# A recurrent-memory attention with a routed MLP on one core: the first step's softmax, left rows and a granule's load rearranged, and the tail's gate and up products turned round

## The chip, the core and the metric

The kernel runs on one core of a Trainium2 chip. Its engines are TensorE (PE in the profile; PEld is its weight load), VectorE (DVE), ScalarE (ACT), GpSimd (POOL) and SyncE (SP), which here only issues DMAs. The metric is the device time of one execution in microseconds; less is better. The time of a kernel is the median of several executions.

## The reference

Inputs are bfloat16. Part A is attention over 64 segments of 32 rows, with 8 memory rows that each segment hands to the next; part B is an MLP on the two rows that a router picks. Cut to what matters:

```python
def _A_ref(x, mem0, Wq, Wk, Wv, Wo, seg_len):   # x (1, 2048, 1024), 32 heads of 128, M = 8 memory rows, seg_len = 32
    ...
    for s in range(n_seg):
        xs = x[:, s * seg_len:(s + 1) * seg_len, :].copy()
        h = jnp.concatenate([mem, xs], axis=1)
        q = jnp.einsum('btd,dhe->bhte', h, Wq)
        ...
        p = _softmax(scores, axis=-1)
        o = jnp.einsum('bhqk,bhke->bhqe', p, v)
        o = jnp.einsum('bhte,hed->btd', o, Wo)
        mem = o[:, :M, :].copy()
        outs.append(o[:, M:, :])
    return jnp.concatenate(outs, axis=1)
def _B_ref(x, w_r, w_gate, w_up, w_down):       # w_gate, w_up (1024, 3584), w_down (3584, 1024)
    ...
    x_sel = jnp.take_along_axis(x, idx_e, axis=1)
    g = _silu(x_sel @ w_gate)
    u = x_sel @ w_up
    y = g * u @ w_down
    ...
xn = _layernorm(x, axis=-1)
return x + _A_ref(xn, A_mem0, A_Wq, A_Wk, A_Wv, A_Wo, A_seg_len) + _B_ref(xn, B_w_r, B_w_gate, B_w_up, B_w_down)
```

## The kernel before

**Main and left rows.** Only what the recurrence needs goes from segment to segment: 8 memory rows and the first 24 rows of the segment, 32 rows in all (ST, one column per row). The last 8 rows of each segment, 512 rows over the 64 segments, are the left rows. They change nothing for the memory, so their queries, keys and values are worked out together in the first segment, dense and 128 wide, their attention runs along with the segments, and their output projection comes in the tail.

**Weights.** Wq, Wk, Wv and Wo are cut into 64 granules of 128 x 2048 (512 KB): 0 to 47 for six phases of q, k and v (PHASES, line 27), 48 to 63 for Wo. 44 granules are resident in SBUF. 17 are streamed again for every segment through five slots (`fetch`, line 383, tile g, queue SP); three more are partly kept in PSUM (KEPT) and brought back by copies. Some rooms are used twice. The room "pair" first holds XLT, the turned left rows; later granules 60 and 61. "big0" holds the raw left rows XLR, then gathered queries and keys (GA), then W8A, then OTA, the left rows' attention output. "big1" holds x, then GA, then W8B, eight granules of Wo. The room of granule 62 (`hm`) holds VG, the left values, in between.

**The start** (lines 619 to 631). `left_stats` takes mean and variance of four tiles of 128 left rows on VectorE and normalises them; `left_turns` transposes them on TensorE, eight blocks a tile, into XLT; `left_qk` then makes a head's queries with eight matmuls of 512 columns (line 506) and ScalarE copies them to GA (line 508). The weights of the first phase come in two halves (`first_half`, line 460).

**The first segment.** Each phase is followed by the same product for the left rows. After a phase of v, `left_v` (line 527) runs four tiles of rows times four column blocks, each of eight matmuls (line 533), copies each block to VG (line 536, ScalarE and VectorE in turn) and stores it to vl_d in HBM (line 537, SP). In the second half it also loads W8B through POOL, and granule 60 once the first two tiles of XLT are used. `scores` (QK products, mask, maximum) is run by a hook at a point of the phases; `exponent` (ScalarE, line 681) and `soften` (VectorE) follow at a later hook. In the first segment the second half's pair stands at hook (4, 7), the last block of phase 4, ahead of VM's copy (line 785) on ScalarE. At a phase's end `left_done` (line 554) fetches the streamed granules that follow and, after phase 5, loads 61 and 62.

**The segments.** Six phases, then the residual (line 358) and sixteen granules of Wo (line 804). PSm's matmuls (line 757) hold 32 columns of weights (ST) and are placed in four column groups of the array, so that four run side by side.

**The tail.** During the last segment's Wo the parts of OTA that the first two blocks of left rows need are loaded (eight loads of 256 KB, `load_left_out`, on POOL), and with each Wo granule one piece of the MLP's weights is fetched (`fetch_moe`, SP, 16 pieces of gate). Then six pieces of up go out and the other eight loads of OTA (SP); the left x rows are loaded on ScalarE's queue. `left_sums` normalises those on VectorE, `left_rows_out(0)` and `(1)` each project two blocks of 128 left rows (64 matmuls of 512 columns a block, line 880, in PSUM WD), add x (line 886) and store them (line 887, POOL). Between the two, `gate_up(0, early)` multiplies the first 20 of 32 pieces, and the rest after. A piece of weights is the stationary operand, 14 blocks of 128 x 128, and the two routed rows are the moving one, two columns wide (line 910); the freed room takes the next piece. Then silu (928), the product (930), and 112 matmuls with w_down (938) into YP. T is the two routed output rows, loaded back from HBM after the left rows are stored (923); line 941 adds YP to them and line 943 stores them.

**Order.** The order of each engine is the order of the program text (`manual_schedule`); each queue's DMAs are issued in that order too. The hardware queues of SP and ScalarE share eight semaphores, so a ninth DMA waits for the first to land.

## Time and profile before

| | us |
|---|---|
| median of 3 runs | 1842.9 (1832.21 to 1852.85) |
| the profiled execution | 1829.7 |
| its span, first to last instruction | 1828.1 |
| PE busy | 1552.2 (85%) |
| DVE, ACT, POOL busy | 878.1, 776.9, 321.0 |
| mean granted PE clock | 0.986 |
| moved by DMA | 678.50 MB, mean 371 GB/s |

All rows of the profile are from one execution. "L506" is line 506. A row of the timeline has the start, the length, engine, line, operation, out<-in, the size and how many were merged, and in brackets the idle time before it with what ended it. A row of a line's or group's view gives count, shortest, median and longest duration in ns and the first and last start. A queue row gives a DMA's form, how many, their size and the median time from issue to landing. The first segment reaches to about 226, the last segment's Wo ends at 1743.8, and the tail is what follows.

### The profile page before, as it was taken

What the parts mean: (1) busy time and instruction counts of PE and PEld (TensorE: products, weight loads), DVE (VectorE), ACT (ScalarE), POOL (GpSimd) and SP (SyncE); (2) the same over time, 40 slices, a digit from 0 to 9 for tenths busy, and PEclk for the clock granted to TensorE, in tenths of its full rate; (3) what the DMA queues carried; (4) which work ended last, traced back from release to release, by engine and by line L of the source; (5) the groups of instructions that cost most, each with busy time, mean ns of one, the idle gap of its engine ahead of it and who ended that gap; (6) DMA issues with size and microseconds to landing.
All of it is one profiled execution on the core that took longest, in us unless ns stands there. A gap on an engine that the chain in (4) does not pass through costs nothing. (4 is left out here: it accounts for less than half of the span.)

```text
span 1828.1 us, 70401 instructions
## 1 busy us (share of the span) xinstructions
PE 1552.2 (85%) x30370; PEld 827.1 (45%) x30370; DVE 878.1 (48%) x2707; ACT 776.9 (42%) x2023; POOL 321.0 (18%) x596
## 2 busy tenths in 40 slices
PE   6999888888888888888888888888888888888888
PEld 3444344444444444444444444444444444444465
DVE  6722254555455555544555455454445555555420
ACT  2342144444444444444444444444444444444400
POOL 1111111111111111111111111111111111111200
PEclk9999899999999999999999999999999999999988
DMA  9785999999999999999999999999999999999996
GB/s 360 274 302 158 308 364 369 395 391 397 375 393 395 395 396 393 379 387 368 397 394 398 384 389 396 369 382 379 383 393 395 395 389 396 397 395 395 389 385 246
DMA packets 219961, 678.50 MB, mean 371 GB/s; under 512 B 46849, under 2 KB 50225, under 8 KB 219649
## 3 DMA queue, kind: packets, MB, share of 16 engines
q1 hardware_dynamic: 193688, 623.79, 89.0%
q0 software_dynamic: 24512, 47.59, 7.6%
q8 instruction: 237, 3.88, 0.9%
q10 hardware_dynamic: 1448, 2.62, 0.4%
q14 instruction: 76, 0.61, 0.1%
HBM read 652.90 MB, written 29.89 MB: 374 GB/s over the span
## 5 line engine op out<-in xcount | busy, mean ns | idle before, releaser
L757 PE MATMUL PSm<-wres,ST 128*32 128x512 bf16 x6400 | 499.9, 382 | 0.0
L757 PEld LDWEIGHTS <-ST 128*32 128x32 bf16 x12288 | 312.3, 96 | 336.7 <-issue 91.4
L757 PE MATMUL PSm<-g,ST 128*32 128x512 bf16 x3080 | 307.1, 384 | 37.0 <-DMA g<-wsc 33.7
L414 ACT COPY BK<-KEPT 128x512 bf16<-128x512 bf16 x315 | 189.2, 601 | 180.3 <-PE WO L804 68.2
L804 PEld LDWEIGHTS <-OT 128*32 128x32 bf16 x8192 | 209.3, 97 | 88.6 <-issue 72.2
L766 ACT CAST XB<-PSm 128x512 bf16<-128x512 f32 x256 | 150.2, 587 | 118.8 <-PE PSm L757 117.4
L804 PE MATMUL WO<-W8B,OT 128*32 128x256 bf16 x4096 | 186.8, 277 | 0.0
L654 DVE COPY KT<-BT 128x512 bf16<-128x512 bf16 x126 | 51.1, 405 | 280.8 <-PE BT L644 276.2
L757 PE MATMUL PSm<-W8A,ST 128*32 128x512 bf16 x2048 | 182.8, 381 | 0.0
L599 POOL DMA_DIRECT2D QKL<-ql_d x63 | 46.5, 737 | 753.3 <-ACT OTL L726 738.5
L804 PE MATMUL WO<-g,OT 128*32 128x256 bf16 x2560 | 130.7, 277 | 55.6 <-DMA g<-wsc 50.1
L838 POOL DMA_DIRECT2D out_dram<-XN x256 | 130.6, 525 | 178.3 <-DVE XN L834 177.9
L785 ACT CAST VM<-PSm 128x512 bf16<-128x512 f32 x128 | 80.1, 625 | 114.3 <-PE PSm L757 114.3
L414 DVE COPY BK<-KEPT 128x512 bf16<-128x512 bf16 x189 | 80.2, 425 | 72.3 <-ACT BK L414 36.6
L644 PEld LDWEIGHTS <-XB 128*128 128x128 bf16 x1024 | 58.0, 98 | 108.7 <-ACT XB L766 102.0
L644 PE MATMUL BT<-IDENT,XB 128*128 128x128 bf16 x1024 | 101.7, 222 | 3.3
L686 DVE TENSOR_REDUCE DN<-BS 128x8 f32<-128x320 f32 x128 | 62.9, 492 | 85.4 <-ACT BS L681 85.4
L671 DVE TENSOR_TENSOR BS<-BS,CT 128x96 f32<-128x96 f32 (+1 forms) x256 | 59.7, 233 | 84.3 <-PE BS L664 79.8
L506 PE MATMUL PSG<-XLT,wres 128*128 128x512 bf16 x352 | 98.7, 382 | 0.8 <-ACT GA L508 0.7
L649 ACT COPY QT<-BT 128x512 bf16<-128x512 bf16 x128 | 74.9, 585 | 52.7 <-PE BT L644 49.2
L757 PE MATMUL PSm<-BK,ST 128*32 128x512 bf16 x567 | 75.3, 387 | 22.5 <-DVE ST L372 22.5
L834 DVE CAST XN<-WO 128x256 bf16<-128x256 f32 x64 | 27.2, 425 | 131.7 <-PE WO L804 131.7
(176 smaller groups left out, 2282.1 us busy)
## 6 DMA issues: line engine op xcount, KB each, us to landing
g<-wsc SPq DMA_DIRECT2D x1071, 512.0 KB, 6.3
ql_d<-GA POOLq DMA_DIRECT2D x16, 512.0 KB, 6.7
QKL<-ql_d POOLq DMA_DIRECT2D x63, 128.0 KB, 6.2
MW<-in_B_w_gate_dram SPq DMA_DIRECT2D x16, 448.0 KB, 8.3
MW<-in_B_w_down_dram SPq DMA_DIRECT2D x14, 512.0 KB, 10.9
wres<-in_A_Wk_dram SPq DMA_DIRECT2D x12, 512.0 KB, 10.7
MW<-in_B_w_up_dram SPq DMA_DIRECT2D x12, 448.0 KB, 9.6
XP<-in_A_x_dram SPq DMA_DIRECT2D x8, 512.0 KB, 10.5
```

Source lines behind the costliest of these rows:

```text
L414: copy(out=back[g][c], in_=KEPT_COLS[g][c])
L506: nc.tensor.matmul(PSG[:, :], lhsT=part(Gs[kc], h // 4)[:, P * (h % 4):P * (h % 4 + 1)], rhs=XLT[:, :, kc, :], start=(kc == 0), stop=(kc = ...
L644: nc.tensor.transpose(out=PTq[:, il, :, :].rearrange("p j r -> p (j r)"), in_=XB[:, il * P:(il + 1) * P], identity=IDENT[:, :])
L649: nc.scalar.copy(out=QT[half][:, :, :], in_=pv)
L654: (nc.vector.tensor_copy if s else nc.scalar.copy)(out=KT[half][:, :, 0:32], in_=pv)
L671: nc.vector.tensor_tensor(out=S4, in0=S4, in1=m, op=ALU.add)
L686: nc.vector.tensor_reduce(out=DN[:, :], in_=S8, axis=AX.X, op=ALU.add)
L757: nc.tensor.matmul(PSm[32 * jq:32 * jq + 32, :], lhsT=ST[:, kc, :], rhs=part(Gv, jq), start=(kc == 0), stop=(kc == KC - 1), tile_position= ...
L766: nc.scalar.copy(out=XB[:, :], in_=PSm[:, :])
L785: nc.scalar.copy(out=VM[half][:, :], in_=PSm[:, :])
L804: nc.tensor.matmul(PS[32 * g:32 * g + 32, 0:256], lhsT=lhs(h), rhs=Gv[:, D * hs + 256 * g:D * hs + 256 * (g + 1)], start=False, stop=(last ...
L838: nc.gpsimd.dma_start(out=out2[s * SEG:s * SEG + XM, 256 * g:256 * (g + 1)], in_=OB[32 * g:32 * g + XM, :])
```

## The change

In the start the left rows go in two pairs: `left_stats` and `left_turns` take a range, and `first_heads` makes the queries of the first four heads in two column halves of 256, in four banks of PSUM (FIRST) that later hold KEPT. `warm_up` runs matmuls on the identity whose result nothing reads: 80 ahead of the first pair, 24 ahead of the second pair's transposes.

In the first segment the second half's `exponent` and `soften` move from hook (4, 7) into `left_v(0)`, after its first tile of rows. In `left_v(1)` the stores of the last two tiles go through POOL, and granule 61 is loaded in two halves, after the third and the fourth tile, where before it followed phase 5.

In the tail four of POOL's eight loads of OTA, and the left x, move to SP, behind the segment's loop and ahead of the remaining fetches. Gate and up hold the two routed rows (RX, padded to 32 columns) as the stationary operand and stream the weights, 448 columns a matmul, in four column groups; the result lies across 32-row groups in four banks, silu and product work on four parts, and seven transposes (HTP) bring it back to columns. w_down is loaded in an order that fits them. `keep_warm` runs 12 and 5 more matmuls that nothing reads. A silu on one unused column is placed ahead of `left_rows_out(1)`.

```diff
+    def warm_up(n):
+        W = psA.tile([P, 512], F32, tag="acc", name="WARM")
+        for _ in range(n):
+            nc.tensor.matmul(W[:, 0:P], lhsT=IDENT[:, :], rhs=IDENT[:, :], start=True, stop=True)
+
+    def first_heads(Gs, c):
+        for h in range(4):
+            for kc in range(KC):
+                nc.tensor.matmul(FIRST[h][:, 256 * c:256 * (c + 1)], lhsT=part(Gs[kc], 0)[:, P * h:P * (h + 1)],
+                                 rhs=XLT[:, 2 * c:2 * c + 2, kc, :], start=(kc == 0), stop=(kc == KC - 1), skip_group_check=True)
+            if c == 1:
+                GA = gathered[0].rearrange("p s (m i q r) -> p s m i q r", m=2, i=4, q=4)
+                nc.scalar.copy(out=GA[:, :, 0, h, 0, :], in_=FIRST[h].rearrange("p (s r) -> p s r", r=XL))
...
-    moe += [("dn", fg) for fg in range(FC // 2)]
+    moe += [("dn", j, gp) for j in range(FC // 4) for gp in range(2)]
...
+                W = B_w_down.rearrange("(f g x) d -> f g x d", f=2, g=4)
+                for f in range(2):
+                    x0, x1 = max(P * j, FQ * f), min(P * (j + 1), FQ * (f + 1))
+                    if x0 < x1:
+                        nc.sync.dma_start(out=t3[x0 - P * j:x1 - P * j, :, :],
+                                          in_=W[f, 2 * gp:2 * gp + 2, x0 - FQ * f:x1 - FQ * f, :].rearrange("a p d -> p a d"))
...
-    def left_v(half, Gs):
+    def left_v(half, Gs, amid=()):
...
-                nc.sync.dma_start(out=vl_d[b][4 * jq:4 * jq + 4, :, :, half, :].rearrange("i s r e -> (s r) i e"),
-                                  in_=VQ.rearrange("p (i e) -> p i e", i=4))
+                (nc.gpsimd if half and b > 1 else nc.sync).dma_start(
+                    out=vl_d[b][4 * jq:4 * jq + 4, :, :, half, :].rearrange("i s r e -> (s r) i e"), in_=VQ.rearrange("p (i e) -> p i e", i=4))
             nc.gpsimd.tensor_copy(out=GATE, in_=VG[:, 1536:1540])
+            if b == 0:
+                for fn in amid:
+                    fn()
...
+                if b > 1:
+                    g = AREAS["pair"][1]
+                    c = slice(D * (b - 2), D * (b - 1))
+                    res_tiles[g] = room(g, "")
+                    nc.sync.dma_start(out=res_tiles[g][:, c], in_=granule_dram(g)[:, b - 2, :])
...
-            for g in AREAS["pair"][1:] + [hm]:
-                load_resident(g)
+            load_resident(hm)
...
-    left_stats()
-    left_turns()
+    warm_up(80)
+    left_stats(0, 2)
+    left_turns(0, 2)
+    first_heads(first_Gs, 0)
+    left_stats(2, 4)
+    warm_up(24)
+    left_turns(2, 4)
     row_stats(xt(0), S6, MV[:, 0, :])
     sd_rows(MV[:, 0:1, :], VE[:, 0:1])
-    left_qk(0, 0, [t for _, t in first_phase], iter(()), 0, 2)
+    gathered[0] = area("big0", [P, NSEG, 256], "GA")
+    first_heads(first_Gs, 1)
     spread(0, 1)
     norm_seg(0)
-    left_qk(0, 0, [t for _, t in first_phase], iter(()), 2, 5)
+    left_qk(0, 0, first_Gs, iter(()), 4, 5)
...
-        hook(*((5, 0) if s else (4, 7)), exponent)
-        hook(*((5, 0) if s else (4, 7)), lambda: soften(1))
+        if s:
+            hook(5, 0, exponent)
+            hook(5, 0, lambda: soften(1))
...
-                    left_v(half, [Gv_ for _, Gv_ in behind])
+                    left_v(half, [Gv_ for _, Gv_ in behind], () if half else (exponent, lambda: soften(1)))
...
-                for k in range(8):
+                for k in range(4):
                     load_left_out(k, nc.gpsimd)
...
-    fetch_moe()
-    for k in range(8, 16):
+    for k in range(4, 8):
         load_left_out(k, nc.sync)
...
-        nc.scalar.dma_start(out=left_x(t), in_=x_left[t, :, XM:SEG, :])
+        nc.sync.dma_start(out=left_x(t), in_=x_left[t, :, XM:SEG, :])
+    fetch_moe()
+    for k in range(8, 16):
+        load_left_out(k, nc.sync)
...
+    GU = [[psA.tile([P, 512], F32, tag="acc", name=f"GA{fh}") for fh in range(2)], [BS, BT]]
+    RX = T2[:, 256:512].rearrange("p (k r) -> p k r", r=32)
+    nc.vector.memset(T2[:, 256:512], 0.0)
+    nc.vector.tensor_copy(out=RX[:, :, 0:2], in_=RXT)
...
-            for fl in range(FC // 2):
-                col = (w * FC + fh * (FC // 2) + fl) * 2
-                nc.tensor.matmul(GU[:, col:col + 2], lhsT=Gt[:, fl * P:(fl + 1) * P], rhs=RXT[:, kc, :],
-                                 start=(w + kc + fh + fl == 0), stop=True, skip_group_check=True)
+            for g in range(4):
+                nc.tensor.matmul(GU[w][fh][32 * g:32 * g + 32, 0:FQ], lhsT=RX[:, kc, :], rhs=Gt[:, FQ * g:FQ * (g + 1)],
+                                 start=(kc == 0), stop=(kc == KC - 1), tile_position=(0, 32 * g), skip_group_check=True)
...
     gate_up(0, early)
+    nc.scalar.activation(out=T2[:, 126:127], in_=T2[:, 124:125], func=ACTF.Silu)
     left_rows_out(1)
...
+    keep_warm(12)
+    HTP = psA.tile([P, 1024], BF16, tag="acc", name="HTP")
+    for j in range(FC // 4):
+        nc.tensor.transpose(out=HTP[:, P * j:P * (j + 1)], in_=HR[:, P * j:P * (j + 1)], identity=IDENT[:, :])
...
+    keep_warm(5)
```

More of the change, by code (lines that the diff above doesn't have):

```diff
@@ L499, in left_qk @@
     def left_qk(mat, half, Gs, between, h0=0, h1=16):
-        if mat == 0 and h0 == 0:
+        if mat == 0 and half and h0 == 0:
             gathered[half] = area(f"big{half}", [P, NSEG, 256], "GA")
@@ L872, with keep_warm @@
     OTR = OTA.rearrange("p s (r h) -> p (s r) h", h=H)
+    def keep_warm(n):
+        W = psK.tile([P, 512], F32, name="WARM", tag="kept0")
+        for i in range(n):
+            nc.tensor.matmul(W[:, 0:256], lhsT=IDENT[:, :], rhs=T2[:, 256:512], start=True, stop=True)
     def left_rows_out(k):
@@ L891 @@
     left_rows_out(0)
-    ROW = T0[:, 0:256]
+    T3 = one.tile([P, 256], BF16, tag="bA", name="T3")
+    ROW = T3[:, 0:256]
     def quarters(c):
-        return T0[c:c + 97:32, 0:256]
+        return T3[c:c + 97:32, 0:256]
     def routed_out(v):
@@ L926 @@
     end_rows = [ends[c].value_load(I8[0:1, c:c + 1], min_val=0, max_val=S - 1) for c in range(2)]
[L927 to L930 removed]
+    HR = T0[:, 0:2 * FQ]
+    SG = [[T0[:, 1024 + 448 * i:1024 + 448 * (i + 1)].bitcast(F32) for i in range(2)],
+          [one.tile([P, 224], F32, tag=tag, name="SG") for tag in ("kt", "bE")]]
@@ L931 @@
+    HT = T2[:, 160:160 + 2 * FC].rearrange("p (j g c) -> p j g c", g=4, c=2)
+    nc.vector.tensor_copy(out=HT, in_=HTP[:, 0:32 * FC].rearrange("p (j g r) -> p j g r", g=4, r=32)[:, :, :, 0:2])
+    keep_warm(5)
     YP = psA.tile([P, 512], F32, tag="acc", name="YP")
     nc.vector.memset(YP[:, 0:256], 0.0)
-    for fg in range(FC // 2):
-        Gt = moe_tiles["dn", fg]
-        for a in range(2):
-            fc = 2 * fg + a
-            for g in range(4):
-                nc.tensor.matmul(YP[32 * g:32 * g + 2, 0:256], lhsT=HT[:, fc, :],
-                                 rhs=Gt[:, a * D + 256 * g:a * D + 256 * (g + 1)], start=(fc == 0), stop=(fc == FC - 1),
-                                 tile_position=(0, 32 * g))
+    for j in range(FC // 4):
+        for gp in range(2):
+            Gt = moe_tiles["dn", j, gp]
+            for a in range(2):
+                for g in range(4):
+                    nc.tensor.matmul(YP[32 * g:32 * g + 2, 0:256], lhsT=HT[:, j, 2 * gp + a, :],
+                                     rhs=Gt[:, a * D + 256 * g:a * D + 256 * (g + 1)], start=(j + gp + a == 0),
+                                     stop=(j == FC // 4 - 1 and gp + a == 2), tile_position=(0, 32 * g))
```

50 lines of the change are left out of this document (28 added, 22 removed).

## The prediction

> **What bounds the kernel now.** I read the page first: the span, the DMA's share in its slices, the chain of waits.
>
> ```profile
> span 1828.1 us, 70401 instructions
> ...
> DMA  9785999999999999999999999999999999999996
> ...
> DMA g<-wsc 4%; PE PSm L757 1%; PE WO L804 1%; DMA VL<-vl_d 0%; PE YP L938 0%; DMA out_dram<-XLS 0%; PE BT L644 0%; ACT QT L649 0%; ACT BS L681 0%; DVE DN L686 0%; DVE KT L654 0%; DVE PT L692 0%; DVE XN L834 0%; DVE PT L696 0%; PE BS L662 0%
> ```
>
> The largest piece of the chain is the streamed weights (g<-wsc), and the DMA is full in nearly all slices. Busy time by stretches shows where it isn't (columns: stretch, length, five engines, PE clock, DMA share, GB/s):
>
> ```profile
> 212.00:216.00 4.00, 2.94 (x89) 2.26 (x89) 2.80 (x12) 1.36 (x5) 0.69 (x2) 1.00 0.66 136
> 408.00:600.00 192.00, 161.96 (x3592) 86.28 (x3596) 97.81 (x313) 89.25 (x240) 35.39 (x64) 1.00 1.02 390
> 1763.00:1773.00 10.00, 10.00 (x50) 6.63 (x49) 0.09 (x1) 0.00 (x0) 0.47 (x1) 1.00 1.03 407
> ```
>
> The loop over segments streams at 390 GB/s with a full DMA, and the change leaves it alone. In the first segment, where the left rows are done too, the DMA has slack and TensorE sets the time: 216 us is where the stream becomes the bound, so what TensorE saves before it shifts all that follows. In the tail both are full. What TensorE waits for between 60 and 300 us (total, times, longest):
>
> ```profile
> PE WO L804 <- DMA g<-in_A_Wo_dram: 4.0, 2, 3.7
> PE PSV L533 <- ACT VM L785: 2.2, 1, 2.2
> ```
>
> **The start.** Two rows of the left pairs are to be normalised, turned and multiplied before the other two.
>
> ```profile
> L240 DVE BATCH_NORM_AGGREGATE MISC<-MISC x4: 209/209/209, 5.7 to 10.4; 128x2 bf16<-128x12 f32 x4
> ```
> ```profile
> L232 PE MATMUL PX<-IDENT,XLR x32: 267/314/315, 11.9 to 15.6; 128*128 128x128 bf16 x32
> ```
> ```profile
> 17.04 1.01 PE L506 MATMUL PSG<-XLT,g 128*128 128x512 bf16 x2 [1.10 <-ACT XLT L233]
> 17.84 1.06 PE L506 MATMUL PSG<-XLT,wres 128*128 128x512 bf16 x2
> ```
> ```profile
> L508 ACT CAST GA<-PSG x4: 585/585/586, 20.3 to 25.6; 128x512 bf16<-128x512 f32 x4
> ```
> ```profile
> 8.19 0.33 SPq L460 DMA_DIRECT2D wres<-in_A_Wq_dram  x1
> ```
> ```profile
> wres<-in_A_Wq_dram SPq DMA_DIRECT2D x1, 256.0 KB, 5.6
> ```
>
> Before, the fourth head is through at 25.6. After, the second aggregate comes at 5.7 + 1.57 = 7.3, the first turn 1.5 later as before (10.4 to 11.9), at 8.8. But the last half granule, issued at 8.19, lands at 13.8, and that holds all heads: 25 half-wide matmuls then remain. At full clock one 512-wide matmul costs 13.60/64 = 0.21 (left rows, below), so half costs 0.106: to 16.5. The 24 warm-up matmuls, a quarter each, add 1.3; turning and copying the second pair half of the 5.1 that four took (11.9 to 17.04), 2.6; 32 more half-wide ones 3.4: 23.8, and 0.3 for the spread that the old order had already passed. Gain 1.5. VectorE's second pair (3.1 of statistics and about 1.5 to the turn, after its copy at about 11.5) is ready at 16 to 17, under TensorE's work. The matmuls at 17 us come two in 0.80, half the full rate. If that clock still held, 57 half-wide ones would cost 0.094 more each: the gain would be a loss of 3.9. If the 24 fell under a wait, it would be 2.8. I take 1.5, since 80 warm-up matmuls precede.
>
> The Trainium skill (TensorE: Matmul & The Clock Gate, Part 1) says that about 3.4 us of activity release the full clock and an idle window of that length takes it away; by it the wait until 13.8 is just short enough and 1.5 stands, and the half-rate pair at 17 us agrees with it.
>
> **The softmax moved.** VM's copy no longer stands behind the exponent on ScalarE, and the 2.2 above goes. Exponent and divisions now stand between ScalarE's and VectorE's copies of left v; each of them copies one product in two, so the work fits in the 3.4 between its copies (two products of 8 x 0.21). If it didn't, it would give back at most the 2.2.
>
> **The stores on POOL and granule 61.**
>
> ```profile
> 207.88 0.58 ACT L536 CAST VG<-PSV 128x512 bf16<-128x512 f32 x1 [5.49 <-DMA vl_d<-VG]
> ```
> ```profile
> 213.39 3.29 SPq L389 DMA_DIRECT2D g<-in_A_Wo_dram  x3
> ```
> ```profile
> 211.75 0.38 PE L533 MATMUL PSV<-g,XLT 128*128 128x512 bf16 x1
> ```
> ```profile
> 224.41 0.62 PE L804 MATMUL WO<-wres,OT 128*32 128x256 bf16 x8 [0.73 <-DMA wres<-in_A_Wo_dram]
> ```
>
> SP's three fetches stood behind the last stores of v and started 1.4 after TensorE had freed the room. Now only half a granule stands there (0.4): 1.0 sooner. Half of 61 leaves this busy stretch: 256 KB at 390 GB/s, 0.7. The load of 62 into VG's room still waits for the last stores. The ScalarE wait at 207.88 stays, since the store now queues on POOL behind three loads of 512 KB. So 1.7 (0 to 2.7, the upper end with that wait shortened by 1.0). New waits: POOL's stores wait for the copies of v, and behind them stand W8B's last two loads and the next segment's QKL, none of them needed before 213; the second half of 61 waits on SP for TensorE's last columns of x, and behind it stand the three fetches (its 0.4 is counted). First segment: 1.5 + 2.2 + 1.7 = **5.4**.
>
> **The tail's loads.**
>
> ```profile
> 1743.11 0.62 PE L804 MATMUL WO<-g,OT 128*32 128x256 bf16 x8 [2.75 <-DMA g<-wsc]
> ```
> ```profile
> OTA<-ol_d POOLq DMA_DIRECT2D x8, 256.0 KB, 9.7
> MW<-in_B_w_gate_dram SPq DMA_DIRECT2D x3, 448.0 KB, 13.9
> XLS<-in_A_x_dram ACTq DMA_DIRECT2D x4, 256.0 KB, 12.6
> ```
> ```profile
> L441 SPq DMA_DIRECT2D MW<-in_B_w_gate_dram x16: 327/330/642, 1733.7 to 1758.6; - x16
> ```
> ```profile
> 1743.66:1759.11 15.45, 15.45 (x64) 9.36 (x65) 0.89 1.04 365
> 1759.11:1772.71 13.60, 13.60 (x64) 9.03 (x63) 1.00 1.03 407
> 1781.24:1796.67 15.43, 15.43 (x65) 9.38 (x65) 0.89 1.04 399
> 1796.67:1810.40 13.73, 13.73 (x65) 9.08 (x63) 1.00 1.01 377
> ```
>
> The last granule shares the DMA with POOL's and ScalarE's loads and lands at 1743.1. With 2 MB of those moved I take 1741.5 (between 1739 and 1743). But four loads of OTA and the left x now stand on SP behind sixteen gate loads, which the segment's loop issues first. At 407 GB/s those 7.34 MB take 18.0 and 1.05 MB of OTA 2.6: OTA is whole at 1762.1. The first row block runs 1742.1 to 1757.5 and TensorE then waits 4.6; the second, cold again, takes 15.45: 1777.6, against 1772.7. The left x land 2.6 after OTA, and their sums, about 10 by the rows (12.6 after some 1738 to VectorE's first sum, at 1761.34 below), end by 1775, under the second block. Behind these loads on SP stand six up pieces and the other eight of OTA: the bytes before them are the same as before, and they are due only at 1783, so nothing is booked for them.
>
> **Gate and up.**
>
> ```profile
> 1761.34 1.28 DVE L886 TENSOR_TENSOR XLS<-XLS,WD 128x512 bf16<-128x512 bf16 x2
> ```
> ```profile
> 1772.71:1781.24 8.53, 7.51 (x282) 0.79 1.04 396
> ```
> ```profile
> 1652.40 1.26 PE PSm L757 x20
> ```
> ```profile
> 1812.05 0.53 POOL L887 DMA_DIRECT2D out_dram<-XLS  x1 [13.28 <-DVE T L921]
> 1816.74 1.23 POOL L923 DMA_DIRECT2D T<-out_dram  x2 [4.16 <-DVE T L930]
> ```
> ```profile
> out_dram<-XLS POOLq DMA_DIRECT2D x4, 256.0 KB, 5.7
> T<-out_dram POOLq DMA_DIRECT2D x2, 2.0 KB, 2.7
> ```
> ```profile
> 1822.74 0.48 DVE L941 SCALAR_TENSOR_TENSOR T<-YP,SIG,T 128x256 bf16<-128x256 f32 x1 [5.77 <-PE YP L938]
> ```
>
> RX is written on VectorE behind the second block's sum: 1.28 and 0.4 for two small ones, so gate and up start at 1779.3. Four column-tiled 512-wide matmuls cost 1.26/5 = 0.25, 448-wide ones 0.22: twenty pieces 4.4 in place of 8.53, to 1783.7. The clock stays up: 2 x 13.65 = 27.3, to 1811.0, against 1810.4. From there two chains lead to L941. By the loads of T, which wait for the last left rows in HBM: 6.3 to the issue as before, 1.23 and 2.7: 1821.2. By TensorE: before 12.3; twelve pieces (2.6) replace 168 small matmuls (168 x 8.53/280 = 5.1): 9.8, so 1820.8; new transposes and warmer matmuls are taken to cancel. The table for silu is loaded early, on a ScalarE that stands idle beside the left rows; if it weren't, 1.3 would return to this chain. Two of the fourteen down loads become two halves each, with the same bytes. L941 starts at 1821.3 in place of 1822.74: **1.4** gained, though gate and up save 6.6. Bounds: at 365 GB/s OTA is 2.4 later and the tail loses 1.0; the upper end is the first rival.
>
> **Sum.** 5.4 + 1.4 = 6.8 off a profiled execution of 1829.7 (1.6 around the span): 1822.9. That execution lies 13.2 below the median of the runs, 1842.9, so the forecast is 1836.
>
> **Rivals.** *The tail's loads interleave.* If OTA arrives by the time it is needed, the second block starts at 1757.5: 1771.1, then 1772.8, 1777.2 and 1804.5. With the DMA still full the store takes 5.7, not 4.7, and L941 starts at 1815.7: 7.0 gained, 12.4 in all, 1830.5. For: loads of three queues did run side by side at 1733 to 1750. Against: these now stand on one queue. The Trainium skill (DMA: Bandwidth & Descriptors, Issuing engines are not separate DMA queues) says that DMAs run on the same sixteen engines and interleave whichever engine started them; taken literally that is this rival, and the rows of three queues show only that different queues share.
>
> *POOL's stores are slow (slower than before).* Eight stores of 512 pieces of 256 B follow W8B's loads on POOL. At s us each they clear at 207.9 - 3.7 + 8s, where TensorE's last copy was due at about 209.2: 8s - 5 late, and 62 and the segment's end with it. From s = 1.5 nothing is left of the gain; at 2.5 it is 15 late, 8.2 slower, 1851. Against:
>
> ```profile
> ol_d<-OTL POOLq DMA_DIRECT2D x64, 64.0 KB, 5.4
> VL<-vl_d POOLq DMA_DIRECT2D x63, 64.0 KB, 6.0
> ```
>
> POOL's transfers in small pieces land like the others. But no row shows 256 B pieces there.
>
> *The stream swallows the first segment's gain.* If the DMA were already the bound before 216, only the tail's 1.4 is left: 1841.5. Against: the 0.66 share at 212.
>
> **Chances.** Forecast 0.50, interleaved loads 0.18, swallowed 0.20, slow stores 0.12. One per cent, about what a measurement tells from no change, is 18 us; the runs lie within 11 of their median. So a run below 1824.5 needs the forecast or the first rival with a low median, or gains I don't see: 0.17. One above 1861 needs the slow stores and a high median: 0.08. Between, 0.75. The forecast alone, by its bounds, spans 1834 (2.8 + 2.2 + 2.7 + 1.4) to 1846 (-3.9 + 2.2 + 0 - 1.0), before scatter. The range goes from the first rival less 10 to the slow stores: 1820 to 1850.
>
> **What would show it.** Right: fourth head done near 24; no wait on VM L785; the fetches at L389 within 0.6 of left v's end; segment 0 about 5 sooner; OTA from SP landing near 1757 (5 earlier, all shifted), TensorE idle for 4 to 5 amid the left rows; gate and up twenty pieces in 4 to 5. Wrong: stores on POOL landing more than 1.5 apart, heads still at half rate after 14 (the warm-up then doesn't do what it says), or no idle time between the left row blocks.

## The result, and the profile after

The changed kernel takes 1837.07 us (median of 20 runs), the kernel before 1839.93 (20 runs beside them): a ratio of 0.9993 with a 95% interval of 0.9971 to 1.0016 (estimated over the runs; the quotient of the two medians is 0.9984), so no change that can be measured. The forecast of 1836 lies 1 us off. But the 6.8 us that it was to gain would be a ratio of 0.9963, which the interval leaves out; the time was hit because the runs of before came out 3 us lower too, and that is luck.

One profiled execution of each, cut at four events (us):

| | before | after | difference |
|---|---|---|---|
| first matmul of left v | 149.68 | 147.66 | -2.0 |
| its second half begins | 182.55 | 178.14 | -4.4 |
| first segment's copy of WO | 225.50 | 220.72 | -4.8 |
| last segment's copy of WO | 1743.78 | 1740.67 | -3.1 |
| last addition (L941, now L1004) | 1822.74 | 1821.45 | -1.3 |
| end of the span | 1828.07 | 1830.10 | +2.0 |

The front gained 4.8; 63 segments of stream took 1.7 of it, the work of the tail 1.8, and the stretch behind the last addition 3.3. The stream's length varies by 18 us from one profile to the next (1516 to 1534 over the kernels below; one profile, of `all_three`, fell into a disturbed execution and isn't compared), so single spans say little and the stages are compared instead.

The start, in the timeline of TensorE (start, length, line, operation, idle time before it and what ended it):

```profile
1.51 6.71 PE L240 MATMUL WARM<-IDENT 128*128 128x128 bf16 x80 [1.51 <-POOL IDENT masks.py:199]
...
11.39 0.38 PE L245 MATMUL FIRST<-XLT,g 128*128 128x256 bf16 x2 [0.88 <-DVE XLT L234]
...
12.27 0.28 PE L245 MATMUL FIRST<-XLT,g 128*128 128x256 bf16 x1 [0.28 <-DMA g<-in_A_Wq_dram]
...
13.51 0.28 PE L245 MATMUL FIRST<-XLT,wres 128*128 128x256 bf16 x1 [0.85 <-DMA wres<-in_A_Wq_dram]
13.63 0.49 PE L245 MATMUL FIRST<-XLT,g 128*128 128x256 bf16 x3
...
16.36 1.50 PE L240 MATMUL WARM<-IDENT 128*128 128x128 bf16 x24
...
19.54 0.39 PE L245 MATMUL FIRST<-XLT,g 128*128 128x256 bf16 x2 [0.79 <-DVE XLT L234]
```

The first heads wait for weights until 13.5 and then run at 0.11 us apiece (13.63 to 13.96 for three), the full rate. The 24 warm-up matmuls stand between them and the second pair.

Who waited for whom, on TensorE between 140 and 222 us (total, times, longest):

```profile
PE WO L842 <- DMA g<-in_A_Wo_dram: 4.2, 2, 2.1
PE PSV L549 <- ACT VG L552: 1.8, 1, 1.8
PE WO L842 <- DMA wres<-in_A_Wo_dram: 1.4, 1, 1.4
```

The wait for VM is gone. The waits for granules of W_o are as long as before (4.0 for g, 0.7 for wres and 1.1 for granule 61, whose own wait is gone).

The tail, by TensorE, VectorE and ScalarE:

```profile
1740.67 0.42 DVE L872 CAST XN<-WO 128x256 bf16<-128x256 f32 x1 [6.17 <-PE WO L842]
```
```profile
1751.40 4.48 PE L925 MATMUL WD<-g,OTA 128*128 128x512 bf16 x19
1762.50 9.38 PE L925 MATMUL WD<-W8B,OTA 128*128 128x512 bf16 x32 [6.61 <-DMA OTA<-ol_d]
...
1780.29 3.21 PE L959 MATMUL GA<-MW,T 128*32 128x448 bf16 x64 [1.51 <-DVE T L951]
...
1784.47 6.85 PE L925 MATMUL WD<-W8B,OTA 128*128 128x512 bf16 x31 [0.21 <-issue]
```
```profile
1821.45 0.48 DVE L1004 SCALAR_TENSOR_TENSOR T<-YP,SIG,T 128x256 bf16<-128x256 f32 x1 [4.67 <-DMA T<-out_dram]
```
```profile
1823.94 1.16 ACTq L1006 DMA_DIRECT2D out_dram<-T  x1
```

TensorE stands 6.6 us between the first two row blocks, waiting for OTA; the twenty gate and up pieces take 4.2 (1780.29 to 1784.47) where 8.5 stood. And the last output is issued at 1823.94, 1.3 before that of before, but the program ends at 1830.1.

Behind that last issue only closing instructions are left, which the page and its views don't list. The trace's own records name them: POOL's DRAIN, an instruction that it runs at the program's end, lasts from 1818.45 to 1829.29, 10.83 us. Before, it ran from 1817.34 to 1825.31, 7.97 us, and SP, drained at 1827.27, ended last. Now SP is drained at 1826.06 and POOL is late.

### The profile page after: what moved, and what is told of

It is laid out like the page before. It is cut to its first block, busy times and chain, and to the rows that moved or that the text cites. A ratio compares the mean times of both kernels' runs of the same rounds, so it can differ in the third digit from the quotient of the medians.

```text
span 1830.1 us, 70088 instructions
## 1 busy us (share of the span) xinstructions
PE 1551.3 (85%) x30198; PEld 830.0 (45%) x30210; DVE 880.2 (48%) x2716; ACT 779.7 (43%) x2028; POOL 325.0 (18%) x600
## 3 DMA queue, kind: packets, MB, share of 16 engines
q10 hardware_dynamic: 872, 1.58, 0.2%
## 5 line engine op out<-in xcount | busy, mean ns | idle before, releaser
L823 ACT CAST VM<-PSm 128x512 bf16<-128x512 f32 x128 | 80.1, 626 | 115.0 <-PE PSm L795 114.9
L522 PE MATMUL PSG<-XLT,wres 128*128 128x512 bf16 x336 | 93.1, 379 | 0.8 <-ACT GA L524 0.7
L348 POOL DMA_DIRECT2D XN<-in_A_x_dram x64 | 34.9, 546 | 311.4 <-PE PSm L795 149.8
```

What stands on the lines that cost most here:

```text
L522: nc.tensor.matmul(PSG[:, :], lhsT=part(Gs[kc], h // 4)[:, P * (h % 4):P * (h % 4 + 1)], rhs=XLT[:, :, kc, :], start=(kc == 0), stop=(kc = ...
L823: nc.scalar.copy(out=VM[half][:, :], in_=PSm[:, :])
```

## The experiments

All are edits of the changed kernel. What each measured stands in the table at the end of this section: L is left v's first matmul, F the time from the start of its second half to the first segment's WO copy, V the time from the last segment's WO copy to the last addition, C from there to the span's end.

**Front and tail alone.**

In `front_only` the last segment's loads and all that follows are the code of before:

```diff
-                for k in range(4):
+                for k in range(8):
                     load_left_out(k, nc.gpsimd)
...
-    GU = [[psA.tile([P, 512], F32, tag="acc", name=f"GA{fh}") for fh in range(2)], [BS, BT]]
+    GU = psA.tile([P, 512], F32, tag="acc", name="GU")
```

In `tail_only` the start, the second softmax and left v are:

```diff
-    warm_up(80)
-    left_stats(0, 2)
...
+    left_stats()
+    left_turns()
```

> The change's front (warm-up matmuls, left rows in two pairs, second softmax amid left v, granule 61 in two parts) with the tail of before. Theory A (front and tail are two separate accounts): the first segment's Wo copy ends at 220.7 +- 0.6 us (225.5 before, 220.7 in the change's own profile), the stretch from the last segment's Wo copy to the span's end stays at 84.3 +- 1.0, and the median is 3 to 5 us below the kernel before (ratio 0.9973 to 0.9984). Rival B (the weight stream, bound by the transfers, swallows the front's gain): the first segment still ends 4.8 sooner, the last segment ends no sooner than in before's profile (1743.8 +- 1), and the ratio is 1.000.

> The change's tail (gate and up as moving operand, left-out rows and left x on SP behind the gates, half-partition w_down loads) with the front of before. Theory A: the first segment ends at 225.5 +- 0.6, the stretch from the last segment's Wo copy to the end is 89.4 +- 1.0 (84.3 before), TensorE idles 5 to 7 us ahead of the second left-row block, POOL's last instruction ends after SP's, and the median is 3 to 6 us above the kernel before (ratio 1.0016 to 1.0033). Rival B (the long tail of the one profile came from the shifted front or from chance): the stretch is 82 to 86 and the ratio is 0.999 to 1.000.

Measured: `front_only` 0.9949 (0.9914 to 0.9983), `tail_only` 1.0000 (0.9971 to 1.0028). By its ratio the front gains, and the 1.000 of rival B, in which the stream swallows the gain, lies outside the interval. Its profile doesn't have the stages of theory A: the WO copy comes at 223.7, not 220.7, since L is 149.5, and from the last WO copy to the end it takes 86.0, not 84.3. The tail shows its idle time (6.70) and a V of 80.1; its span's end, 86.6 after the WO copy, is neither theory's, and its ratio is rival B's. The 89.4 of the change's profile was a V like this one plus a later close. In `front_only`, with the old tail, C is 6.1 and POOL's DRAIN 11.16 long; in `tail_only` the DRAIN takes 7.65. So its length came with the front.

**T's loads from SP.**

```diff
-    for c in range(2):
-        nc.gpsimd.dma_start(out=quarters(c), in_=routed_out(routed_rows[c]))
...
+    sp_rows = [end_rows[0], nc.sync.value_load(I8[0:1, 1:2], min_val=0, max_val=S - 1)]
+    for c in range(2):
+        nc.sync.dma_start(out=quarters(c), in_=routed_out(sp_rows[c]))
```

> The two loads of the routed rows T issued by SP instead of POOL. In the change's profile SP is drained at 1826.1 us and the span ends with POOL at 1829.3, which issued these loads at 1817.8. Theory A (POOL's closing stretch counts from its last transfer): POOL's last transfer is now the left rows' store at about 1813.4, POOL ends 3 to 5 us sooner than before, SP ends last, and the stretch from the last segment's Wo copy to the end goes from 89.4 to 86 or 87. Rival B (POOL's closing stretch has a length of its own, or counts from the end of all other engines): POOL still ends last, at 88 to 90. Rival C: SP's own reading of the row number puts the T loads 1 to 2 us later, and what POOL gives is lost there.

POOL's DRAIN starts at 1818.09, with the issue of the last store, is 10.60 long, and ends at 1828.68, with SP at 1829.21: C is 5.22, as before the change. That is theory A, with 84.9 from the WO copy to the end, a little below its 86 to 87, and rival C isn't seen (V 79.7).

**The late loads early.**

```diff
             if w == 2 and s + 1 == NSEG:
...
+                for k in range(4, 8):
+                    load_left_out(k, nc.sync)
+                XLS = [room(resident[k], "XLS") for k in range(2)]
+                for t in range(4):
+                    nc.sync.dma_start(out=XLS[t // 2][:, D * (t % 2):D * (t % 2 + 1)], in_=x_left[t, :, XM:SEG, :])
```

> The second four left-out row loads and left x go out on SP when the last segment's third granule of gates is called for, ahead of most gate and up loads, in place of behind the last gate. Theory A (the late loads are the cost): the 6.6 us idle of TensorE ahead of the second left-row block goes to under 1.5, this block starts at 1756 to 1757 instead of 1762.5, the last left-row block ends 4 to 6 us sooner, and the stretch from the last segment's Wo copy to the end goes from 89.4 to 84 to 86. Rival B (the transfers bound the tail as they do the stream): the same bytes in another order leave the last w_down load landing at 1816 or so; the left rows end sooner, but TensorE then waits for w_down, and the stretch stays at 88 to 90. Rival C: the loads take the last segment's own weights' place and the last segment ends 2 us or more later.

```profile
1747.91 0.42 DVE L877 CAST XN<-WO 128x256 bf16<-128x256 f32 x1 [6.96 <-PE WO L842]
```
```profile
1757.87 4.48 PE L925 MATMUL WD<-g,OTA 128*128 128x512 bf16 x19
1762.19 7.07 PE L925 MATMUL WD<-W8B,OTA 128*128 128x512 bf16 x32
...
1821.37 0.39 PE L1001 MATMUL YP<-MW,T 128*2 128x256 bf16 x8 [0.89 <-DMA MW<-in_B_w_down_dram]
```
```profile
1822.98 0.48 DVE L1004 SCALAR_TENSOR_TENSOR T<-YP,SIG,T 128x256 bf16<-128x256 f32 x1 [6.14 <-DMA T<-out_dram]
```
```profile
1825.46 1.16 ACTq L1006 DMA_DIRECT2D out_dram<-T  x1
```

The second block follows the first without a pause, and it runs warm: 7.07 for its first 32 matmuls where the pause made it 9.38. V falls by 5.7, to 75.07. Rival B has a part: TensorE now waits 0.9 for the last w_down load. From the last WO copy to the end it takes 84.8, as theory A said, where the changed kernel took 89.4; the span is no shorter, since the stream took 4.3 longer in this profile. POOL's DRAIN ends it and takes 1.1 of the gain: 7.2 us lie between the last issue and 1832.7. That made the next question.

**What POOL's closing time counts.**

In `stores_on_sp`:

```diff
-                (nc.gpsimd if half and b > 1 else nc.sync).dma_start(
+                nc.sync.dma_start(
```

In `pool_free` the left rows' stores go out on ScalarE, T's loads on SP and ScalarE, and the silu of the gate half stands ahead of the second pair of row blocks:

```diff
-            nc.gpsimd.dma_start(
+            nc.scalar.dma_start(
                 out=out2.rearrange("(t s r) d -> t s r d", t=4, s=16)[2 * k + b, :, XM:SEG, :], in_=x)
...
+    for c in range(2):
+        ends[c].dma_start(out=quarters(c), in_=routed_out(end_rows[c]))
```

> The changed kernel with all of left v's stores back on SP's queue (eight fewer POOL transfers, granule 61 and the fetches queued behind them). In the six profiles so far POOL's closing stretch lasts 7.6 to 8.0 us with the old front and 10.6 to 11.2 us with the new one, and what the new front adds on POOL is these eight stores. Theory A (POOL's closing stretch grows with what POOL issued): it lasts 7.5 to 8.0 us, and the stretch from the last segment's Wo copy to the span's end is 85.5 to 87 (89.4 in the change's profile). Rival B (the length is chance): 10.5 us or more again. For the front, theory A: from left v's first matmul to the first segment's Wo copy 73.0 to 73.6 us, as in the changed kernel's four profiles (73.0 to 74.2); rival C, by the prediction's third term: 74.4 to 75.0.

> The changed kernel with the stores of the left rows on ScalarE's queue and the two loads of T on SP's and ScalarE's (POOL's last transfer is then the last segment's output, near 1743 us); the activation of the gate half stands ahead of the left rows' second half for that. Theory A (POOL's closing stretch runs from its last issued transfer): it is over near 1754 us, the span ends with SP, and the stretch from the last Wo copy to the end is 84.5 to 86 (SP was drained 85.4 after the copy in the change's profile). Rival B (the closing stretch begins when the other engines end): POOL ends last again, 88 or more. Rival C: ScalarE's queue delivers T 1 us or more later, and the stretch is 86 to 87.

```profile
1837.79 1.15 ACTq L1006 DMA_DIRECT2D out_dram<-T  x1
```
```profile
core 0: 1840.7 us, clock 0.986
```

In `stores_on_sp` the DRAIN takes 7.64 us, and the end comes 2.9 after the last issue, as in the kernel before (1825.20 and 1828.1). The front loses nothing: F is 42.3, where the stores on POOL gave 42.1 to 43.9, so the stores had no need to leave SP. In `pool_free` the DRAIN starts at 1750.31, takes 10.62 beside the left rows, and C is 5.29. Both theories A hold: the DRAIN starts with the issue of POOL's last transfer and waits for no other engine, and the eight stores make it 3.2 longer.

**A first version of mends.** Early loads, no POOL transfer in the tail, and gate, up and down cut so that no w_down load has 64 partitions:

```diff
-    FQ = F // 8
+    FS = (512, 384)
...
-                for f in range(2):
-                    x0, x1 = max(P * j, FQ * f), min(P * (j + 1), FQ * (f + 1))
...
+                f, x0 = j // 4, P * (j % 4)
+                W = B_w_down[2048 * f:2048 * f + 4 * FS[f], :].rearrange("(g x) d -> g x d", g=4)
+                nc.sync.dma_start(out=t3, in_=W[2 * gp:2 * gp + 2, x0:x0 + P, :].rearrange("a p d -> p a d"))
```

> Three mends of the tail together: left-out rows and left x early on SP, no POOL transfer after the last segment's output, and gate, up and down cut in 512 and 384 columns per group, so that no w_down load has 64 partitions only. Theory A (the tail's loss is these three things): the left rows run without an idle over 1 us between their first two blocks; the last w_down load lands 3 to 5 us sooner after the last Wo copy than in the run with early loads alone (73.4); POOL ends before SP; the stretch from the last Wo copy to the end is 78 to 80.5 us (84.3 and 86.0 with the old tail), and the median is 5 to 9 us below the kernel before (ratio 0.995 to 0.997). Rival B (the last store of the left rows and T behind it set the end): the stretch is 81 to 83. Rival C (the stream's spread hides it): the stretch is as in A and the ratio's interval holds 1.000.

The ratio is 0.9964 (0.9934 to 0.9993), but the mechanism failed: from the last WO copy to the end its profile, the one set aside above, has 82.2, rival B's value. SP's timeline, one row per group of issues (start, time from first to last):

```profile
1784.41 9.34 SPq L451 DMA_DIRECT2D MW<-in_B_w_up_dram  x6
1793.85 9.62 SPq L627 DMA_DIRECT2D OTA<-ol_d  x8
```

In the trace SP issues nothing between 1785.70 and 1792.00 and between 1795.57 and 1801.71. ScalarE issued a left rows' store at 1785.55 and another at 1794.28; they take their places among the eight semaphores that the two queues share, and the load that resumes each time uses the store's own semaphore. `pool_free` has such a stop too, 4.1 us from 1811.75, and there the trace has the landing: ScalarE's store landed at 1815.78 and SP went on at 1815.84, with the store's semaphore. With the stores back on POOL (below) the stops are gone. The last w_down load lands 76.1 after the WO copy here and 70.4 in `mended`; how much of that the stops made isn't shown.

**The warm-up.**

`no_warm` leaves out both lines, `no_24` the second.

```diff
-    warm_up(80)
...
-    warm_up(24)
```

> The changed kernel without the 80 and 24 warm-up matmuls. In the profiles of the new front left v's first matmul starts at 147.7, 147.9, 149.5 and 150.4 us, and the two late ones have first heads of 0.21 us a matmul from 13.9 or 14.5 us on, after a wait on a weight, in place of 0.11. Theory A (the start is set by whether TensorE is warm when the first heads run): without the warm-up the first heads take 0.21 for 3 us or more, and left v starts at 149.5 to 151. Rival B (the landing of the first weights sets it): the heads start as late as before, and left v starts at 147.5 to 148.5.

> The changed kernel without the second warm-up alone (24 matmuls, 1.34 us in the change's profile, between the first and the second pair of left rows); the first 80 stay. Theory A (these 24 lie on the path and warm nothing, since the first heads ran at full rate just before): from the end of the first pair's heads to the second pair's first head 2.3 us in place of 3.2, the heads that follow at 0.11 a matmul. Rival B (without them the clock falls): the second pair's heads run at 0.21 and end later than with them. The first pair's heads end at 16.3 to 16.6 us if the first weights land by 12.5, at 18 to 19 us if TensorE waits for them twice.

Without either, the first heads do run at 0.21 (eleven of them), and yet left v starts at 146.96, sooner than both theories say: the ratio is 0.9948 (0.9918 to 0.9979). In `no_24`:

```profile
13.43 0.28 PE L245 MATMUL FIRST<-XLT,wres 128*128 128x256 bf16 x1 [0.99 <-DMA wres<-in_A_Wq_dram]
13.55 0.49 PE L245 MATMUL FIRST<-XLT,g 128*128 128x256 bf16 x3
...
16.28 1.06 PE L233 MATMUL PX<-IDENT,XLR 128*128 128x128 bf16 x16
18.12 0.39 PE L245 MATMUL FIRST<-XLT,g 128*128 128x256 bf16 x2 [0.79 <-DVE XLT L234]
```

From the end of the first pair's heads to the second pair's first head it takes 1.84, against 3.18 with the 24 (16.36 to 19.54), and the clock stays up. In all eleven profiles of the new front in the table, left v starts 131.3 us after the end of the first pair's heads with the 24, and 129.96 without them: they cost 1.34 and warm nothing. What varies is that end, from 16.3 to 19.5, with the clock and with x's arrival. `loads_early` had the same 80, and waits of 1.11 and 0.75:

```profile
12.94 0.39 PE L245 MATMUL FIRST<-XLT,g 128*128 128x256 bf16 x1 [1.11 <-DMA g<-in_A_Wq_dram]
...
14.29 0.39 PE L245 MATMUL FIRST<-XLT,wres 128*128 128x256 bf16 x1 [0.75 <-DMA wres<-in_A_Wq_dram]
14.48 0.85 PE L245 MATMUL FIRST<-XLT,g 128*128 128x256 bf16 x3
```

0.85 for three there, 0.49 in `no_24`. The time of `no_24` doesn't show its start: 1.001 (0.9978 to 1.0042).

**All mends together.** No warm-up, left v's stores on SP, loads early, 512 and 384 columns, T from SP; then the same with the change's 448 columns:

> The changed kernel with five mends: no warm-up matmuls at the start, left v's stores on SP's queue, left-out rows and left x early, gate, up and down cut in 512 and 384 columns, T's loads on SP; the left rows' stores stay on POOL (on ScalarE's queue they took one of the eight semaphores shared with SP, and SP stood still for 6 us twice). Theory A: left v starts at 147 to 148 us, the first segment's Wo copy is at 219.5 to 221, no idle over 3 us stands between left-row blocks, the last w_down load lands at most 70 us after the last Wo copy, POOL's closing stretch is about 7.6 us and over before SP's, and the stretch from the last Wo copy to the end is 77 to 79.5 us (84.3 before, 89.4 in the change's profile); ratio to the kernel before 0.990 to 0.994. Rival B (the same bytes bound the tail): the last w_down load still lands 73 us or more after the Wo copy and the stretch is 81 or more. Rival C (the stream returns the front's gain): the tail is as in A and the ratio is 0.995 to 0.998.

> The kernel with the five mends less one: gate, up and down keep the change's 448 columns, so four of the w_down loads have 64 partitions. Theory A (these loads slow the transfers around them): the last w_down load lands 72 to 74 us after the last Wo copy, 3 to 4.5 us later than with 512 and 384 columns, TensorE waits for it at the end, and the stretch from the Wo copy to the end is 2 to 4 us longer than there. Rival B (they only wait in a full queue): the two land alike, within 1 us.

```profile
1751.39 4.48 PE L920 MATMUL WD<-g,OTA 128*128 128x512 bf16 x20
1755.71 7.07 PE L920 MATMUL WD<-W8B,OTA 128*128 128x512 bf16 x32
...
1778.48 7.10 PE L920 MATMUL WD<-W8B,OTA 128*128 128x512 bf16 x32 [3.31 <-DMA OTA<-ol_d]
```

`mended` gives 0.9929 (0.9895 to 0.9964), 1824.82 us against 1837.67; `mended_halves` 0.9882 (0.9830 to 0.9934), from four runs, 1817.23. Both intervals lie below 1 and below that of the changed kernel (0.9971 to 1.0016), which ran beside other runs of before. V is 74.3 and 73.6, C 5.35 and 5.23; from the last WO copy to the end it takes 79.6 and 78.8, at the edge of theory A's 77 to 79.5. L is 149.4 and 148.9, since the first turns began at 10.3 and 10.5 us and the cold heads ended near 19: theory A's start was wrong. 3.3 us of idle are left ahead of the third block, now for OTA's second half.

The columns made no difference that can be told. GB/s in 40 slices of some 2 us from 1740 on, `mended`:

```profile
GB/s 387 391 256 267 273 353 402 410 401 404 401 412 408 418 404 401 390 408 373 365 392 412 407 410 393 388 391 386 401 390 388 389 389 383 174 8 2 1 1 0
```

and `mended_halves`:

```profile
GB/s 392 330 261 287 326 407 406 403 404 406 407 405 419 404 407 392 398 398 405 400 411 404 408 394 388 388 389 392 257 250 237 372 387 389 293 28 1 1 1 0
```

The w_down loads of 64 partitions are the dip to 237 in the second row, about 6 us long, which the first doesn't have. The last w_down load lands 1.5 later (71.9 after the WO copy, against 70.4), between theory A's 3 and rival B's 1, and V doesn't follow.

**The moved loads undone.**

```diff
-                for k in range(4):
+                for k in range(8):
                     load_left_out(k, nc.gpsimd)
...
-        nc.sync.dma_start(out=left_x(t), in_=x_left[t, :, XM:SEG, :])
+        nc.scalar.dma_start(out=left_x(t), in_=x_left[t, :, XM:SEG, :])
```

> One part of the change undone: the first eight left-out row loads on POOL and left x on ScalarE's queue, as in the kernel before; gate and up stay the moving operand. Theory A (the change's tail is two accounts: the moving operand gains, the loads put behind the gates on SP lose): TensorE's idle ahead of the second left-row block is under 1.5 us (6.6 in the change's profile, 6.7 to 7.4 in five others), and SP is drained 79 to 81 us after the last Wo copy, as with early loads (79.7), against 83.5 and 84.4 with the old tail and 84.1 to 85.4 with the change's. Rival B (the gain of the moving operand is lost elsewhere): no idle, and SP drained at 83 or more. In both POOL's closing stretch is 11 us and ends the span later still, since POOL has four transfers more.

```profile
1759.71 4.48 PE L923 MATMUL WD<-g,OTA 128*128 128x512 bf16 x20
1764.03 7.07 PE L923 MATMUL WD<-W8B,OTA 128*128 128x512 bf16 x32
...
1779.52 3.21 PE L957 MATMUL GA<-MW,T 128*32 128x448 bf16 x64 [1.51 <-DVE T L949]
```
```profile
1821.78 0.48 DVE L1002 SCALAR_TENSOR_TENSOR T<-YP,SIG,T 128x256 bf16<-128x256 f32 x1 [5.77 <-DMA T<-out_dram]
```

No idle time stands ahead of the second block; SP is drained 78.5 after the WO copy, V is 74.10: theory A. C is 10.1, with a DRAIN of 11.15. The ratio is 0.9970 (0.9941 to 0.9998).

The stages of the profiles (us), and the ratios to the kernel before:

| kernel | L | F | V | C | POOL's transfers | its DRAIN | ratio |
|---|---|---|---|---|---|---|---|
| before | 149.68 | 42.95 | 78.97 | 5.32 | 573 | 7.97 | 1 |
| tail_only | 148.16 | 42.88 | 80.11 | 6.53 | 569 | 7.65 | 1.0000 |
| front_only | 149.52 | 43.67 | 79.88 | 6.12 | 581 | 11.16 | 0.9949 |
| after | 147.66 | 42.58 | 80.79 | 8.65 | 577 | 10.83 | 0.9993 |
| t_on_sp | 147.87 | 42.43 | 79.70 | 5.22 | 575 | 10.60 | 0.9962 |
| stores_on_sp | 149.14 | 42.31 | 81.05 | 5.41 | 569 | 7.64 | 0.9979 |
| pool_free | 149.41 | 42.29 | 79.55 | 5.29 | 571 | 10.62 | 0.9966 |
| no_warm | 146.96 | 42.05 | 80.53 | 7.91 | 577 | 10.83 | 0.9948 |
| no_24 | 146.24 | 43.17 | 78.58 | 9.35 | 577 | 10.83 | 1.0010 |
| loads_early | 150.42 | 42.74 | 75.07 | 9.73 | 577 | 10.83 | 0.9986 |
| old_loads | 148.18 | 43.89 | 74.10 | 10.11 | 581 | 11.15 | 0.9970 |
| mended | 149.40 | 42.34 | 74.29 | 5.35 | 567 | 7.95 | 0.9929 |
| mended_halves | 148.87 | 42.49 | 73.57 | 5.23 | 567 | 9.00 | 0.9882 |

Added up without the stream (L, the time to the second half of left v, F, V and C), the stages make 309.8 us before, 310.2 in the changed kernel, 309.7 in `front_only`, 307.9 in `no_warm`, 307.8 in `no_24`, 301.9 in `mended` and 300.6 in `mended_halves`. The ratios scatter by more than their intervals tell: `no_warm` and `no_24` lie 0.1 apart by these sums and 11 us by their ratios, and `front_only`, with a ratio of 0.9949, has the sum of before. The mends gain 8 and 9 us by the stages and 13 and 20 by the medians; the rest isn't explained.

## Why the prediction was right, and where it was wrong

The time came out as forecast, by luck; the sum behind it did not: 6.8 were to be gained, and outside the stream 0.4 were lost in the two profiles. With means in place of single values for the start and the tail's work it is 1.5 (2.4 gained by the softmax, 0.6 lost in the tail's work and 3.3 at the close; each below).

**The start, 1.5.** 2.0 in this profile, but that is the spread of the clock. In the seven profiles with both warm-ups L lies between 147.7 and 150.4, 148.9 in the mean, and with the old start it is 149.7 and 148.2, 148.9 too: nothing is gained. The bounds (-3.9 to 2.8) held. The step that failed is "I take 1.5, since 80 warm-up matmuls precede": the 80 don't secure the clock that the heads meet. By the trace's clock records it fell to half for 3.4 us or more in four of the seven (`front_only`, `stores_on_sp`, `pool_free`, `loads_early`). The old start varies alike: full clock from 19.8 us in `before`, from 15.3 in `tail_only`. So the 1.5 compares an old start that happened to be cold with a warm new one; cold against cold it is 149.7 and 149.1 to 150.4, warm against warm 148.2 and 147.7 to 148.2. That the 24 cost 1.3 was right to the digit.

**The softmax, 2.2.** Right: between L and the second half 32.87 us before and in `tail_only`, 30.48 in every profile with the new front, 2.39 less.

**Stores on POOL and granule 61, 1.7.** About nothing: F is 42.9 with the old front, 42.1 to 43.9 (mean 42.9) with the new one and its stores on POOL, and 42.3 to 42.5 with these on SP. The fetches did go out 0.4 after left v's end, as forecast, and the first granule landed sooner; but TensorE waits as long for the granules in all (4.2 and 1.4, against 4.0, 0.7 and 1.1). What the sum left without a price is the load of granule 62, which "still waits for the last stores". Among SP's waits between 205 and 217 us (L138 is the load of 62):

```profile
SPq L138 <- DMA vl_d<-VG: 5.7, 1, 5.7
```

In the changed kernel the last store, issued by POOL at 209.12 behind SP's three fetches, landed at 215.62, 6.5 later, and granule 62 went out at 215.95. Over the profiles 62 goes out 7.5 to 9.5 us after left v's last matmul starts with the stores on POOL, and 4.7 to 5.6 with them on SP.

**The first segment's gain carries through 1:1.** Neither shown nor refuted by spans: the stream's own spread is several times the 2.4 at stake. `front_only` speaks for it, since its interval leaves out 1.000; yet its interval means a gain of 3 to 16 us, and its stages add up to those of before.

**OTA's landing, 4.6 idle.** Right in kind, too small. It came 22.4 after the last granule (1739.96 to 1762.36), where 20.6 was forecast, and TensorE stood 6.6. The term assumed 407 GB/s to the end; by stretches (the last two columns are the DMA's share and GB/s) the changed kernel shows:

```profile
1740.00:1756.00 16.00, 15.46 (x70) 9.40 (x71) 0.42 (x1) 0.00 (x0) 2.02 (x4) 0.90 1.03 405
1756.00:1763.00 7.00, 0.50 (x2) 0.29 (x3) 0.00 (x0) 0.00 (x0) 0.00 (x0) 0.81 1.07 302
```

The gates pass at 405; the second row, with the last 2 us of the gates, OTA and left x, has 302 with the DMA as full. The gates took 18.2 us, as forecast (18.0); OTA's four loads then took 4.2 in place of 2.6. Why these move at a lower rate wasn't tried. The bound of "2.4 later" held.

**Gate and up, 4.4.** Measured 4.2. The moving operand is worth what the sum gave it, and more for the rest of the chain: with the loads in their old places V falls from 79.4 (mean of the two old tails) to 74.1, by 5.3. The moved loads take 5.9 back, to 80.0 (mean of seven, 78.6 to 81.1). So the tail's work loses 0.6, no more than this spread, and 1.8 in the pair of the first table. The forecast had 1.4 gained, but 1.6 of that was to come ahead of V, from the last granule landing sooner; within V it booked a loss of 0.2. That granule took 9.7 us from issue to landing before and 8.9 after: 0.8.

**The end of the program.** Not in the sum at all, and the largest error: "1.6 around the span" was taken as fixed. C grew by 3.3, from two causes. The eight stores lengthen POOL's DRAIN by about 3.2 (7.64 to 10.83). And it starts 3.0 us ahead of the last addition, where it started 5.4 ahead: POOL issues T's loads last, and the last addition now waits for T. Either alone costs less, since before the change the DRAIN ended 2.0 ahead of SP's: C is 6.1 in `front_only` (the stores alone) and 6.5 in `tail_only` (the late start alone). The rival of slow stores had looked for their price at 208 us. Seven of the eight landed by 209.7, the first four 0.4 to 0.8 apart from 203.7 us on; the eighth is the one that holds granule 62 (above).

**The first rival, interleaving loads.** It didn't happen: OTA landed at 1761.3 and 1762.4, after the last gate (1758.2) and ahead of the left x (1763.2), in the order of issue. No run here shows transfers of one queue pass each other. Loads in time were to gain 7.0 in the tail, 5.4 of it within V; they gained 4.4 and 5.3 there (V of 75.07 and 74.10 against 79.4), with the last store 6.2 on its way in `loads_early` where 5.7 was assumed.

## What to carry to other kernels

Putting loads behind others on one queue to clear the way for the earlier ones sets a date for the later ones: work out when the last byte ahead of them has passed, and at which rate they themselves move. Count the program's end as a stage of its own: each store moved to POOL gained nothing where it ran and cost 0.4 us of closing time. Ask of a store that moves what waits for its landing. And the warm-up between two pieces of real work was paid for in full, so let one stand only where the engine would wait.

## What the runs showed of the hardware

POOL's DRAIN starts within 0.2 us of the issue of POOL's last transfer, and waits for no other engine. It took 7.64 and 7.65 us after 569 transfers, 7.97 after 573, and with the eight stores of left v among them 10.60 after 575, 10.83 after 577 (four times), 11.15 and 11.16 after 581: by the differences 0.08 for an ordinary one and 0.4 for each of these stores, which write pieces of 256 B. Where it began beside a full DMA it was longer than these counts give: 7.95 and 9.00 after 567 (`mended`, `mended_halves`) and 10.62 after 571 with the eight stores (`pool_free`).

The clock can fall after short waits, and the same waits don't always do it. After waits of 0.33 and 0.99 (`no_24`) the first heads ran at full rate; after 0.29 and 1.05 (`pool_free`) sixteen of them ran at half rate. The trace's clock records change in steps of 3.41 us: in `pool_free` the granted clock is 1.0 from 7.37 us, 0.5 from 14.20 and 1.0 again from 17.61. In the 3.41 us ahead of the falls TensorE was idle for 1.58 to 2.35 in all (four profiles); at most 1.74 passed without a fall (`no_24`). The two ranges overlap, so this sum alone doesn't settle it. The Trainium skill (TensorE: Matmul & The Clock Gate, Part 1) says that activity is judged in a window of about 3.4 us that runs freely, so that the same kernel meets it at another phase each time; the spread and the steps of 3.41 us agree. It says too that an idle window of that length takes the clock away; in `pool_free` no wait behind the 80 matmuls was longer than 1.05 us, so less idle time is enough.

Loads of 64 partitions pull the whole queue down: 237 to 257 GB/s in three slices, 383 to 401 around the same time where the loads have 128.
